# Narrowing float64 weights: the sign bit from GpSimd as a signed zero, and two VectorE steps per tile in place of three

## The chip, the cores and the metric

The kernel runs on one core of one Trainium2 chip. The metric is device time in microseconds (us) of one execution; lower is better. Engines are named as the profile names them: PE is TensorE's matmul and PEld its weight load, DVE is VectorE, ACT is ScalarE, POOL is GpSimd, SP is SyncE, which issues most of the DMAs here.

## The reference

Two attention steps with a small packed set `p` per batch and head (8 batches, 8 heads, 576 rows, 64 columns) are followed by a maxout layer and a softplus layer on all 4608 rows:

```python
p_packed = sm_attn(p, k, v)
out = sm_attn(q, p_packed, p_packed)
...
h = np.maximum(np.maximum(x @ w1, x @ w2), x @ w3)
return (h @ w_out).astype(np.float32)
...
h = x @ w_in
g = np.maximum(h, 0.0) + np.log1p(np.exp(-np.abs(h)))
return (g @ w_out).astype(np.float32)
```

The six weight matrices (`w1`, `w2`, `w3` and `w_out` of the maxout layer, `w_in` and `w_out` of the softplus layer) come in as float64. The kernel has no 64-bit arithmetic, so it reads each number as two 32-bit words and makes a float32 of them itself. That step is called narrowing below, and the change is in it alone.

## The kernel before

A weight tile is 128 partitions by 512 numbers. It lands by DMA in a buffer of pool `stp` (5 buffers) as pairs of words, `raw[:, :, 0]` the low ones and `raw[:, :, 1]` the high ones, so either word alone is read with a step of 8 bytes. ScalarE's `rebase` (L79) reads the high word as a float32 and scales it by 2^-112, which moves the exponent to float32's place and leaves the mantissa three bits too far to the right. VectorE's `narrow` then does three steps: L86 shifts the rebased bits left by three into the high word's place, L89 adds the top three bits of the low word to that, and L97 takes the sign from the rebased value and all other bits from the sum. The buffer is free for the next load after L97.

Fifty-six tiles are narrowed. Eighteen are `w1` to `w3` (the raw tile is named `wraw`, the result stands in `wsb`); tile fw below, such as 32, is block f (0 to 5) of matrix w (0 to 2). Six are `w_out` of the maxout layer (`woraw`, result `wo`), each then split into a high and a low float32r part (`wo_hi` by ACT at L107, `wo_lo` by DVE at L108). These 24 belong to the first 110 us, where a string `order` lists steps by name and gives the order in which they are emitted. The other 32 (`raw`, result `x`) are the softplus layer's weights, narrowed six per batch in the stage that follows (L628 to L632 store and load them) and written back to HBM.

A scheduler places the emitted instructions on each engine's queue, and each queue then runs strictly in its order. The PE work around the change is this. `scores` (L247) makes scores; `attn1_exp` takes their maximum on DVE (L262), scales it (L266, output `ms`) and lets ACT take the exponential (L271). `attn1_transpose` (L286) and `attn1_values` (L306) follow, and DVE divides by the sums (L320, output `pp`); PE transposes `pp` (L231) before it goes on. `packed_weights` (L375, output `ps_w`) multiplies four tiles of `wsb` at a time; group c takes the tiles 4c to 4c+3, counted as 3f+w, so group 2 needs tiles 22, 30, 31 and 32 and group 3 tiles 40, 41, 42 and 50. ACT and DVE split `ps_w` into `pwhi` and `pwlo`. Layer 1 (L396) multiplies with them; its results are evacuated as `m` by ACT (L419) and by DVE (L421, a running maximum), and split into `hhi` and `hlo`. Layer 2 multiplies with `wo_hi` and `wo_lo`. From batch 1 on this repeats about every 59 us; after batch 7, from some 560 us to the end, the softplus layer runs alone.

Of the kernel before, what the change touches and what calls it, by code (L numbers as in the profile page):

```python
# [8 lines left out]
F32 = mybir.dt.float32  # L9
# [3 lines left out]
ALU = mybir.AluOpType  # L13
# [6 lines left out]
def packed_attention_maxout_softplus(  # L20
# [22 lines left out]
    nc = tc.nc  # L43
# [38 lines left out]

    def narrow(raw, x):

        low, high, bits = raw[:, :, 0], raw[:, :, 1], x.bitcast(I32)
        nc.vector.tensor_scalar(  # L86
            out=high, in0=bits, scalar1=3, scalar2=None, op0=ALU.logical_shift_left
        )
        nc.vector.scalar_tensor_tensor(  # L89
            out=high,  # L90
            in0=low,
            scalar=29,
            in1=high,
            op0=ALU.logical_shift_right,
            op1=ALU.bitwise_or,
        )
        nc.vector.scalar_tensor_tensor(  # L97
            out=bits,
            in0=bits,
            scalar=-0x80000000,  # L100
            in1=high,
            op0=ALU.bitwise_and,
            op1=ALU.bitwise_or,
        )

# [359 lines left out]
    def split_wo(f, t):  # L465
        x = mp.tile([P, S], F32, tag="m", name="wo32")
        rebase(t, x[:, :DM])
        narrow(t, x[:, :DM])
        split(x[:, :DM], wo_hi[:, f], wo_lo[:, f])
# [11 lines left out]
    def narrow_w(f, w, t):  # L481
        x = wsb[:, 3 * f + w].rearrange("p c x -> p (c x)")
        rebase(t, x)
        narrow(t, x)
# [137 lines left out]
    def narrow_ahead():  # L622
        if len(in_flight) == AHEAD or not to_narrow and in_flight:
            raw64, dst = in_flight.pop(0)
            x = nwp.tile([P, 512], F32, tag="x32", name="x32")
            rebase(raw64, x)
            narrow(raw64, x)
            nc.sync.dma_start(out=dst, in_=x)  # L628
        if to_narrow:
            src, dst = to_narrow.pop(0)  # L630
            t = stp.tile([P, 512, 2], I32, tag="st", name="raw64")
            nc.sync.dma_start(out=t.rearrange("p n t -> p (n t)"), in_=src)  # L632
            in_flight.append((t, dst))

    for n in range(1, B):
        for slot in range(F1 + KC):
# [21 lines left out]
            if n + 1 == B:  # L658
# [17 lines left out]
                for c, e in [divmod(lot + i, KC) for i in range(2)] if lot is not None else ():  # L676
                    if e == 0:
# [8 lines left out]
                        out=x, in_=wi32[e * P : e * P + P, c * 512 : c * 512 + 512]  # L686
# [177 lines left out]
```

## Time and profile before

| | |
|---|---|
| Time, median of 3 runs | 1338.73 us (1338.31 to 1339.14) |
| The profiled execution, its own time | 1341.63 us |
| Its span, first to last instruction | 1339.8 us |
| PE busy | 1304.5 us, 97% |
| DVE busy | 894.2 us, 67% |
| ACT busy | 617.9 us, 46% |
| POOL busy | 0.7 us, 6 instructions |
| Mean granted clock of PE | 0.993 |

The page sums over the whole span. PE is busy almost throughout, so what counts is where it is not, and which engine's instruction ends each of these gaps; that is read from the waits and from the timeline of the stretch in question. The table by stretches gives for each engine its busy time, the count of instructions in brackets, and the granted clock of PE, 1.00 being the full 2.4 GHz.

### The profile page before, as it was taken

How to read it: one execution, taken by the hardware profiler on the slowest of the kernel's cores; microseconds unless marked ns; L12 is line 12 of the kernel's file. 1: busy time of each engine (PE TensorE's matmuls, PEld its weight loads, DVE VectorE, ACT ScalarE, POOL GpSimd, SP SyncE). 2: the span in 40 equal slices, each digit the busy share in tenths (PEclk: the TensorE clock that was granted, in tenths of full speed). 3: DMA queues.
4: the chain of work that ended last, by engine and by line, in shares of the span. 5: the costliest groups of instructions: out<-in, count | busy, mean ns of one | idle time of the engine just before them, and what ended most of it. 6: DMA issues, size and time to landing. Idle time of an engine off the chain costs nothing.

```text
span 1339.8 us, 21462 instructions
## 1 busy us (share of the span) xinstructions
PE 1304.5 (97%) x8656; PEld 1100.2 (82%) x8656; DVE 894.2 (67%) x1480; ACT 617.9 (46%) x1045; POOL 0.7 (0%) x6
## 2 busy tenths in 40 slices
PE   4889999999999999999999999999999999999998
PEld 3778888898989899788888888888888888888887
DVE  4787778786878746866556566565665665655654
ACT  3544434444443435745445454454444544544443
POOL 0000000000000000000000000000000000000000
PEclk9979999999999999999999999999999999999999
DMA  9873677877577506501102011010020110000101
GB/s 269 214 197 92 170 202 180 208 212 204 178 201 201 134 36 215 159 0 38 26 1 64 0 32 32 0 47 17 4 60 0 32 32 0 24 8 1 32 1 32
DMA packets 61859, 119.17 MB, mean 89 GB/s; under 512 B 11072, under 2 KB 28736, under 8 KB 61760
## 3 DMA queue, kind: packets, MB, share of 16 engines
q1 hardware_dynamic: 55984, 106.66, 29.8%
q10 hardware_dynamic: 5776, 11.14, 2.5%
q8 instruction: 68, 1.11, 0.3%
q14 instruction: 31, 0.25, 0.1%
HBM read 90.51 MB, written 27.26 MB: 88 GB/s over the span
## 4 chain that ended last, share of the span: by engine, by line
PE 89%; DMA 5%; DVE 3%; ACT 1%; issue 1%; SPq 0%; DVEq 0%; ACTq 0%
PE ps L396 55%; PE acc L781 10%; PE acc L780 10%; PE acc L779 10%; PE ps_w L375 2%; DMA wraw<-in_moe_w_dram 1%; DMA wi_x<-wi 1%; PE ps_s L247 1%; PE ps_v L306 1%; PE ps_e L286 1%; DMA x2d<-xs 1%; DMA kraw<-in_k_dram 1%; DMA vt<-in_v_dram 1%; PE ps_k L199 1%; DVE pwlo L108 0%
## 5 line engine op out<-in xcount | busy, mean ns | idle before, releaser
L396 PE MATMUL ps<-x2hi,wilo 128*128 128x512 f32 x576 | 228.0, 396 | 0.0
L396 PE MATMUL ps<-x2lo,wihi 128*128 128x512 f32 x576 | 227.0, 394 | 0.0
L396 PE MATMUL ps<-x2hi,wihi 128*128 128x512 f32 x576 | 226.7, 394 | 0.0
L781 PE MATMUL acc<-w2hi,glo 128*128 128x512 f32 x576 | 226.0, 392 | 0.0
L780 PE MATMUL acc<-w2lo,ghi 128*128 128x512 f32 x576 | 225.7, 392 | 0.0
L779 PE MATMUL acc<-w2hi,ghi 128*128 128x512 f32 x576 | 224.5, 390 | 0.7 <-ACT ghi L107 0.7
L107 ACT ACTIVATE ghi<-t 128x512 fp32r<-128x512 f32 x144 | 91.0, 632 | 289.0 <-DVE t L761 288.6
L754 DVE TENSOR_SCALAR t<-ex 128x512 f32<-128x512 f32 x144 | 61.4, 426 | 161.9 <-ACT ex L751 161.9
L108 DVE TENSOR_TENSOR glo<-t,ghi 128x512 fp32r<-128x512 f32 x144 | 99.7, 692 | 92.6 <-ACT ghi L107 92.5
L396 PE MATMUL ps<-a2hi,pwhi 128*128 128x288 f32 x576 | 129.3, 307 | 2.5 <-ACT a2hi L107 1.3
L779 PEld LDWEIGHTS acc<-w2hi,ghi 128*128 128x128 f32 x576 | 108.2, 188 | 25.8 <-ACT ghi L107 1.2
L396 PEld LDWEIGHTS ps<-x2lo,wihi 128*128 128x128 f32 x576 | 108.1, 188 | 25.8
L396 PEld LDWEIGHTS ps<-x2hi,wilo 128*128 128x128 f32 x576 | 108.3, 188 | 25.2
L750 ACT ACTIVATE ex<-ps 128x512 f32<-128x512 f32 x144 | 86.2, 598 | 92.3 <-PE ps L396 92.2
L780 PEld LDWEIGHTS acc<-w2lo,ghi 128*128 128x128 f32 x576 | 108.1, 188 | 25.0
L396 PEld LDWEIGHTS ps<-x2hi,wihi 128*128 128x128 f32 x576 | 108.1, 188 | 24.5
L781 PEld LDWEIGHTS acc<-w2hi,glo 128*128 128x128 f32 x576 | 108.1, 188 | 23.5 <-DVE glo L108 0.4
L396 PE MATMUL ps<-a2lo,pwhi 128*128 128x288 f32 x576 | 124.3, 298 | 0.7 <-DVE a2lo L108 0.7
L396 PE MATMUL ps<-a2hi,pwlo 128*128 128x288 f32 x576 | 124.2, 297 | 0.0
L757 DVE TENSOR_TENSOR t<-ln,t 128x512 f32<-128x512 f32 x144 | 99.7, 692 | 30.4 <-ACT ln L752 30.4
L396 PEld LDWEIGHTS ps<-a2hi,pwhi 128*128 128x128 f32 x576 | 93.1, 192 | 15.8 <-ACT m L419 5.9
L761 DVE SCALAR_TENSOR_TENSOR t<-ps,t 128x512 f32<-128x512 f32 x144 | 99.5, 691 | 4.7
(90 smaller groups left out, 1847.9 us busy)
## 6 DMA issues: line engine op xcount, KB each, us to landing
qraw<-in_q_dram SPq DMA_DIRECT2D x112, 140.0 KB
kraw<-in_k_dram SPq DMA_DIRECT2D x96, 140.0 KB
wraw<-in_moe_w_dram SPq DMA_DIRECT2D x18, 512.0 KB
x2d<-xs ACTq DMA_DIRECT2D x32, 288.0 KB
x2r<-x2d SPq DMA_DIRECT2D x36, 256.0 KB
out_dram<-o SPq DMA_DIRECT2D x136, 64.0 KB
raw<-in_moe_w_in_dram SPq DMA_DIRECT2D x16, 512.0 KB
raw<-in_moe_w_out_dram SPq DMA_DIRECT2D x16, 512.0 KB
```

What stands on the lines that cost most here:

```text
L107: nc.scalar.activation(out=hi, in_=src, func=AF.Copy)
L108: nc.vector.tensor_tensor(out=lo, in0=src, in1=hi.bitcast(F32), op=ALU.subtract)
L199: nc.tensor.matmul(ps[64 * G : 64 * G + 64, i // hi, c : c + rows], r[:, i, G], ident[:rows, :rows], start=True, stop=True,)
L375: nc.tensor.matmul(ps[cols, G, : units * P].rearrange("p (w x) -> p w x", w=units), ppT[n][rows, cols], wsb[rows, 4 * c : 4 * c + units, g ...
L396: nc.tensor.matmul(o, w, xx, start=first, stop=last)
L750: nc.scalar.activation(out=ex, in_=ps, func=AF.Abs)
L754: nc.vector.tensor_scalar(out=t, in0=ex, scalar1=1.0, scalar2=-1.0, op0=ALU.add, op1=ALU.add)
L757: nc.vector.tensor_tensor(out=t, in0=ln, in1=t, op=ALU.subtract)
L761: nc.vector.scalar_tensor_tensor(out=t, in0=ps, scalar=0.0, in1=t, op0=ALU.max, op1=ALU.add)
L779: nc.tensor.matmul(ps, ghi[:, cols], whi, start=(f == 0), stop=False)
L780: nc.tensor.matmul(ps, ghi[:, cols], wlo, start=False, stop=False)
L781: nc.tensor.matmul(ps, glo[:, cols], whi, start=False, stop=(f == F2 - 1))
```

## The change

Instead of L86, GpSimd multiplies the high word, read as a float32, by 0.0 in place, once `rebase` has read it: what remains is a zero with the number's sign. L89 adds the top three bits of the low word to this and writes the sum to the low word's place. L97 shifts the rebased bits left by three, which drops their sign, and adds the sum. VectorE has two instructions per tile in place of three, GpSimd has one, and L89 waits for GpSimd.

```diff
         low, high, bits = raw[:, :, 0], raw[:, :, 1], x.bitcast(I32)
-        nc.vector.tensor_scalar(
-            out=high, in0=bits, scalar1=3, scalar2=None, op0=ALU.logical_shift_left
-        )
+        zero = high.bitcast(F32)
+        nc.gpsimd.tensor_scalar(out=zero, in0=zero, scalar1=0.0, scalar2=None, op0=ALU.mult)
         nc.vector.scalar_tensor_tensor(
-            out=high,
+            out=low,
             in0=low,
             scalar=29,
             in1=high,
...
             out=bits,
             in0=bits,
-            scalar=-0x80000000,
-            in1=high,
-            op0=ALU.bitwise_and,
+            scalar=3,
+            in1=low,
+            op0=ALU.logical_shift_left,
             op1=ALU.bitwise_or,
```

PE's instructions keep their order. On DVE and ACT the scheduler places the work around the narrowing anew. Three places are shown, each as before and then as changed; names are as in the section on the kernel, with the program's buffer numbers.

DVE, in the first 35 us, where the maxima of batch 1's first scores (`mx`, `ms`) meet the second `wo` tile (`wo_258`). Before:

```order
L262 TENSOR_REDUCE mx<-ps_s 128x1
L86 TENSOR_SCALAR woraw<-wo_258 128x512
L266 TENSOR_SCALAR ms<-mx 128x1
L262 TENSOR_REDUCE mx<-ps_s 128x1
L89 SCALAR_TENSOR_TENSOR woraw<-woraw 128x512
L266 TENSOR_SCALAR ms<-mx 128x1
L315 TENSOR_SCALAR sg<-es 128x1
L97 SCALAR_TENSOR_TENSOR wo_258<-wo_258,woraw 128x512
```

The same stretch of DVE's queue as changed:

```order
L262 TENSOR_REDUCE mx<-ps_s 128x1 x2
L89 SCALAR_TENSOR_TENSOR woraw<-woraw 128x512
L266 TENSOR_SCALAR ms<-mx 128x1 x2
L97 SCALAR_TENSOR_TENSOR wo_258<-wo_258,woraw 128x512
L315 TENSOR_SCALAR sg<-es 128x1
L319 RECIPROCAL rc<-sg 128x1
L108 TENSOR_TENSOR wo_lo<-wo_258,wo_hi 128x512
```

The first `ms`, which stood ahead of this tile's L89, now stands behind it, and `wo_lo` has moved up ahead of the next tile's steps. On ACT, `wo_hi` of this tile has moved ahead of the second exponential.

DVE, around 77 to 84 us, between the two `pwlo` of group 2 and the last tile that group 3 needs (tile 50). Before:

```order
L86 TENSOR_SCALAR wraw<-wsb 128x512
L108 TENSOR_TENSOR pwlo<-ps_w,pwhi 128x512
L89 SCALAR_TENSOR_TENSOR wraw<-wraw 128x512
L421 TENSOR_TENSOR m<-ps_813,m 128x576
L86 TENSOR_SCALAR wraw<-wsb 128x512
L97 SCALAR_TENSOR_TENSOR wsb<-wsb,wraw 128x512
L421 TENSOR_TENSOR m<-ps_828,m 128x576
L89 SCALAR_TENSOR_TENSOR wraw<-wraw 128x512
L86 TENSOR_SCALAR wraw<-wsb 128x512
L97 SCALAR_TENSOR_TENSOR wsb<-wsb,wraw 128x512
```

The same stretch as changed:

```order
L89 SCALAR_TENSOR_TENSOR wraw<-wraw 128x512
L108 TENSOR_TENSOR pwlo<-ps_w,pwhi 128x512
L89 SCALAR_TENSOR_TENSOR wraw<-wraw 128x512
L421 TENSOR_TENSOR m<-ps_813,m 128x576
L97 SCALAR_TENSOR_TENSOR wsb<-wsb,wraw 128x512 x2
L421 TENSOR_TENSOR m<-ps_828,m 128x576
L89 SCALAR_TENSOR_TENSOR wraw<-wraw 128x512
```

The last L97 of the first listing, tile 50's, has moved ahead of the maximum `m<-ps_828`, and its L89 ahead of `m<-ps_813`. Some 8 us ahead of this, tile 31's L89, which stood before the maximum `m<-ps_730`, now stands behind it together with tile 32's.

DVE, around 86 to 89 us, where the results of batch 1's first attention step (`pp`) are made. Before:

```order
L108 TENSOR_TENSOR hlo<-m,hhi 128x576
L108 TENSOR_TENSOR pwlo<-ps_w,pwhi 128x512
L97 SCALAR_TENSOR_TENSOR wsb<-wsb,wraw 128x512
L86 TENSOR_SCALAR woraw<-wo_962 128x512
L108 TENSOR_TENSOR pwlo<-ps_w,pwhi 128x512
L320 TENSOR_SCALAR pp<-ps_v,rc 128x64 x2
```

The same stretch as changed:

```order
L108 TENSOR_TENSOR hlo<-m,hhi 128x576
L108 TENSOR_TENSOR pwlo<-ps_w,pwhi 128x512
L89 SCALAR_TENSOR_TENSOR wraw<-wraw 128x512
L320 TENSOR_SCALAR pp<-ps_v,rc 128x64
L108 TENSOR_TENSOR pwlo<-ps_w,pwhi 128x512
L97 SCALAR_TENSOR_TENSOR wsb<-wsb,wraw 128x512
L320 TENSOR_SCALAR pp<-ps_v,rc 128x64
```

The two `pp` are now apart, with the second `pwlo` and tile 52's L97 between them.

## Rows read from the trace of the kernel before

**Rows 1.** The page: the span, the busy time of each engine, and the granted clock of PE in 40 slices of 33.5 us.

```profile
span 1339.8 us, 21462 instructions
PE 1304.5 (97%) x8656; PEld 1100.2 (82%) x8656; DVE 894.2 (67%) x1480; ACT 617.9 (46%) x1045; POOL 0.7 (0%) x6
PEclk9979999999999999999999999999999999999999
```

**Rows 2.** Busy time by stretches: the stretch, its length, then PE, PEld, DVE, ACT and POOL busy (instructions), the granted clock, the DMA share and GB/s.

```profile
160.00:480.00 320.00, 318.43 (x3279) 287.28 (x3278) 253.57 (x440) 131.71 (x233) 0.00 (x0) 1.00 0.68 183
480.00:560.00 80.00, 79.27 (x556) 71.08 (x555) 50.91 (x81) 45.01 (x80) 0.00 (x0) 1.00 0.45 148
560.00:1340.00 780.00, 775.78 (x3362) 630.85 (x3360) 477.05 (x752) 371.51 (x608) 0.00 (x0) 1.00 0.08 23
```

**Rows 3.** What PE waited for, over the whole span: us in total, times, longest.

```profile
PE ps_w L375 <- DVE wsb L97: 4.9, 2, 2.6
PE ps_t L231 <- DVE pp L320: 2.1, 2, 1.3
PE ps_s L247 <- DVE vT L223: 1.2, 4, 0.3
PE ps L396 <- DVE hlo L108: 0.5, 1, 0.5
```

**Rows 4.** The removed instruction L86 on the 32 late tiles and on the 18 `wsb` tiles, and the step L89, which stays, on the latter: count, shortest, median and longest in ns, and when the first and last started.

```profile
L86 DVE TENSOR_SCALAR raw<-x x32: 374/422/453, 152.3 to 461.8; 128x512 int32<-128x512 int32 x32
L86 DVE TENSOR_SCALAR wraw<-wsb x18: 417/423/430, 13.6 to 84.2; 128x512 int32<-128x512 int32 x18
L89 DVE SCALAR_TENSOR_TENSOR wraw<-wraw x18: 682/693/695, 14.0 to 85.1; 128x512 int32<-128x512 int32 x18
```

**Rows 5.** The timeline of POOL, three of its six instructions: start, us, and what it was.

```profile
0.24 0.10 POOL L842 MEMSET const-float32-0.0<- 128x1 f32 x1 [0.24 <-issue]
...
0.73 0.20 POOL masks.py:197 MEMSET ident<- 128x128 f32 x1 [0.29 <-POOLq L842]
1.01 0.29 POOL masks.py:199 TENSOR_SCALAR_AFFINE_SELECT ident<-ident 128x128 f32<-128x128 f32 x1
```

**Rows 6.** The timeline from 29 to 40 us, all engines: the first place of the change.

```profile
29.57 0.66 ACT L79 ACTIVATE wo<-woraw 128x512 f32<-128x512 f32 x1 [2.38 <-DMA woraw<-in_moe_w_out_dram]
...
30.61 0.15 DVE L266 TENSOR_SCALAR ms<-mx 128x1 f32<-128x1 f32 x1
...
30.87 0.76 ACT L271 ACTIVATE e<-ps_s,ms 128x576 f32<-128x576 f32 x1
31.34 0.68 DVE L89 SCALAR_TENSOR_TENSOR woraw<-woraw 128x512 int32<-128x512 int32 x1
...
35.20 2.79 PE L306 MATMUL ps_v<-vt,e1T 96*32 96x64 f32 x96 [0.26 <-ACT e1T L292]
...
35.75 0.69 ACT L79 ACTIVATE wsb<-wraw 128x512 f32<-128x512 f32 x1
...
38.86 0.28 DVE L320 TENSOR_SCALAR pp<-ps_v,rc 128x64 f32<-128x64 f32 x1
...
39.29 0.45 PE L231 MATMUL ps_t<-ident,pp 128*128 128x128 f32 x1 [1.29 <-DVE pp L320]
```

**Rows 7.** The timelines of DVE, ACT and PE around groups 2 and 3 of the packed weights, in that order.

```profile
69.18 0.76 DVE L421 TENSOR_TENSOR m<-ps,m 128x576 f32<-128x576 f32 x1 [0.71 <-PE ps L396]
...
72.17 0.69 DVE L97 SCALAR_TENSOR_TENSOR wsb<-wsb,wraw 128x512 int32<-128x512 int32 x1
...
79.74 0.76 DVE L421 TENSOR_TENSOR m<-ps,m 128x576 f32<-128x576 f32 x1 [0.67 <-PE ps L396]
80.42 0.42 DVE L86 TENSOR_SCALAR wraw<-wsb 128x512 int32<-128x512 int32 x1
80.75 0.68 DVE L97 SCALAR_TENSOR_TENSOR wsb<-wsb,wraw 128x512 int32<-128x512 int32 x1
81.35 0.75 DVE L421 TENSOR_TENSOR m<-ps,m 128x576 f32<-128x576 f32 x1
...
82.95 0.68 DVE L97 SCALAR_TENSOR_TENSOR wsb<-wsb,wraw 128x512 int32<-128x512 int32 x1
...
77.17 0.58 ACT L107 ACTIVATE pwhi<-ps_w 128x512 fp32r<-128x512 f32 x1
...
78.72 1.22 ACT L79 ACTIVATE wsb<-wraw 128x512 f32<-128x512 f32 x2
...
73.01 1.96 PE L375 MATMUL ps_w<-wsb,ppT 64*32 64x512 f32 x16 [2.34 <-DVE wsb L97]
...
83.78 1.96 PE L375 MATMUL ps_w<-wsb,ppT 64*32 64x512 f32 x16 [2.59 <-DVE wsb L97]
```

**Rows 8.** What followed the second of these waits: the stretch from 83.78 us by busy time and clock (columns as in rows 2), and the timeline of DVE and PE at its end.

```profile
83.78:92.83 9.05, 8.29 (x127) 6.42 (x128) 7.14 (x14) 1.71 (x4) 0.00 (x0) 0.50 1.04 251
...
88.61 0.47 DVE L320 TENSOR_SCALAR pp<-ps_v,rc 128x64 f32<-128x64 f32 x2
...
89.23 0.45 PE L231 MATMUL ps_t<-ident,pp 128*128 128x128 f32 x1 [0.76 <-DVE pp L320]
```

**Rows 9.** The timeline at the last two `wo` tiles, DVE and then PE.

```profile
107.33 0.76 DVE L86 TENSOR_SCALAR woraw<-wo 128x512 int32<-128x512 int32 x2
...
113.61 0.53 PE L396 MATMUL ps<-hlo,wo_hi 128*128 128x288 f32 x2 [0.48 <-DVE hlo L108]
```

## The prediction

> **What bounds the kernel now.** I read the page first. PE is busy 1304.5 of 1339.8 us, so all that any change outside PE can win is the 35.3 us in which it is idle, and what its clock loses: one slice in 40 stands at 0.7 of full speed [rows 1]. Then the table by stretches, to see where the idle time lies. From 160 to 480 us it is 1.6 us, from 480 to 560 us 0.7, from 560 to the end 4.2 [rows 2]; the other 28.8 us lie before 160 us. Of the 56 narrowed tiles 32 belong to the stretch with 1.6 us of idle time, and there DVE itself is busy 253.6 of 320 us, so it has room already. The 24 tiles of the first 110 us are what can matter. Last the waits of PE: two waits for a last narrowing step of `wsb`, 4.9 us together, two for `pp`, 2.1, and one for `hlo`, 0.5 [rows 3]. These 7.5 us are the places where narrowing stands ahead of PE, directly or by filling DVE's queue. I go through them one by one.
>
> **What the parts cost.** Removed: 56 L86 at 0.42 us [rows 4], 23.6 us of DVE's 894. Nearly all of it lies beside other work. The steps that stay keep their shape and their 0.69 us; back to back they start 0.60 us apart (80.75 to 81.35) [rows 7]. Added: 56 GpSimd multiplications of 128x512. No row shows one, so I bound it by the POOL rows there are [rows 5]. A memset takes 0.10 us for one element per partition and 0.20 for 128, which gives 0.10 + 4 x 0.10 = 0.50 us for 512; the affine select, which also reads, takes 0.29 for 128, which gives 0.10 + 4 x 0.19 = 0.86, or 1.16 if nothing of it is fixed. I take 0.86, since it is the one that reads a tile, and keep 0.50 and 1.16. The Trainium skill (GPSIMD Engine Reference, section Performance versus the Vector engine) gives 769 ns for 512 elements of a one-input loop at its best; by that the sum below would be about 0.1 us lower, since only the first place waits for this length alone. So for one tile alone the path from `rebase` to the result becomes longer (0.86 in place of 0.42, and one more hand-over), while DVE's queue becomes shorter. Which of the two counts depends on whether DVE is late or idle when the tile comes.
>
> **First place, 29 to 39 us.** Here DVE's new order costs. The second `wo` tile is rebased at 29.57, so GpSimd would have its sign from 30.3 to about 31.15. Its L89 now stands ahead of both `ms`, so DVE waits for GpSimd, runs L89 from 31.2, and makes the first `ms` at 31.85 in place of 30.61 [rows 6]. The exponential that it releases moves from 30.87 to 31.95. Behind it on ACT stand a rebase, `wo_hi`, the second exponential, another rebase and the two copies of `e1T`, and PE's `ps_v`, which began at 35.20, would begin near 36.15 and end near 38.95. DVE, meanwhile, is less behind: tile 10's rebase comes at about 36.1 (35.75 before), its sign at 37.65, its two steps end at 38.9, and the second `pp` comes at about 39.1 in place of 38.86. PE's transpose would start near 39.5, not 39.29: **+0.2 us**, between -0.2 (a sign step of 0.50) and +1.0 (no slack on ACT). PE passes this on to all that follows.
>
> **Second place, groups 2 and 3.** From the maximum at 69.18 on [rows 7] the new order is: two L89 at 69.85 and 70.45, L97 of tile 31 at 71.05, a maximum at 71.65, L97 of tile 32 at 72.3. Before, that L97 started at 72.17; group 2 gains nothing (+0.15), because tile 31's first step no longer uses the idle time ahead of 69.18. Group 3 gains. Both steps of tile 40, `hlo`, tile 41's steps, the two `pwlo` and tile 42's L89 take DVE to about 78.65; tile 50's rebase now stands ahead of ACT's copy of `m`, right behind the `pwhi` of 77.17 (0.25 us later now, with the DVE work it waits for), so it runs from 78.0 to 78.65 (from 78.72 before), and its sign is there at 79.55. Then L89, the maximum (79.74 before, 80.15 now), and the two L97 at 80.8 and 81.4. The last one before was that of 82.95, because a maximum, another tile's L86 and this tile's own L86 and L89 stood in between. Group 3 would start at 82.25 in place of 83.78. Most of these 1.5 us are lost again 5 us on: PE's `ps_v` ends 1.5 us sooner, but the two `pp` are now apart, with a `pwlo` and an L97 between them, and that `pwlo` needs ACT, which needs the first `pwlo`. I get the second `pp` at 88.25 to 88.55 and PE's transpose at 88.7 in place of 89.23 [rows 8]: **-0.55 us** in all, between +0.5 and -1.5.
>
> **Third place, the last two `wo` tiles.** Two L86, 0.67 us by their starts (107.33 to 108.00), stand in a queue that is full until `hlo`, for which PE waits 0.48 us [rows 9]. The signs can be ready by 107.5, since both tiles are rebased before DVE comes to them. The gain is the whole wait and no more: **-0.5 us**, between 0 and -0.5.
>
> **The 32 tiles after 150 us.** DVE is freed of 13.5 us, which PE's 1.6 us of idle time [rows 2] caps; what it waits for there on DVE is `vT`, 1.2 us [rows 3]. I take -0.3, between 0 and -1.2. Stores of `x` wait longer by the sign step's length, and loads behind them on SP's queue with them, but no wait of PE for a load is among the 1.6 us.
>
> **Sum.** 0.2 - 0.55 - 0.5 - 0.3 = -1.15 us. Against the profiled execution, 1341.6 us (span 1339.8 and 1.8 around it), that is 1340.5; it lies 2.9 us above the median of the runs, so for the median I say 1338.73 - 1.15 = **1337.6 us**. With all the lower ends together it is 1335.3 (-3.4), with all the upper ones 1340.2 (+1.5). About 0.2%, 2.7 us, is what a measurement of this kernel can tell from no change, so the forecast is "same".
>
> **Rival 1, slower: GpSimd's step holds up DVE's.** L89, L97, `hlo` and `wo_lo` each read two tiles from SBUF. If such an instruction and the sign step could not read at once, each step that falls into a full stretch of DVE's queue would hold it for 0.86 us, twice what the removed L86 took. No row can show it: POOL ends at 1.3 us [rows 5], and DVE's first such step (L89, 14.0 us) comes long after [rows 4]. I count the signs that fall into a full queue ahead of a wait of PE: three before 38.86, one before 72.17, four from there to 88.61, two at 107: ten. If half of them meet a two-input step, that is 5 x 0.86 = 4.3 us, 1337.6 + 4.3 = **1341.9 us**; if all ten do, 1346. It decides the sign from a hold of about 0.5 us on five steps on (4 us would be 0.8 each for a measurable loss). The Trainium skill (SBUF — State Buffer, section Who interferes with whom) says just this: a DVE instruction with two SBUF inputs and a GpSimd instruction that reads SBUF exclude each other, and the later one waits for the whole of the other. What speaks against its weight is that many neighbours in these stretches (the maxima, `pwlo`) read one input from PSUM, and that ACT's and PE's waits leave holes. Chance 0.27.
>
> **Rival 2, faster: the clock.** After the 2.59 us wait before group 3 the granted clock stood at 0.50, the 1.2 GHz level, for 9 us [rows 8]; the 9.05 us from 83.78 to 92.83 would take 4.5 at 2.4 GHz. That wait began at 83.78 - 2.59 = 81.19; the forecast shortens it to 82.25 - 81.19 = 1.06 us. If the clock then stays up, 4.5 us more are won: 1337.6 - 4.5 = **1333.1 us**. Against it: group 2's wait of 2.34 us stays, its `ps_w` ran at the same 1.96 us as group 3's [rows 7], and the wait for `pp` behind `ps_v` becomes longer by about as much as the one before group 3 becomes shorter. Chance 0.2.
>
> **Rival 3: the step is far longer than the rows bound.** At 1.5 us or more it would be late at each place and the gains above would go: +1 us, within "same". Chance 0.05, leaving 0.48 for the forecast.
>
> **How the numbers follow.** The forecast's own range is 1335.3 to 1340.2. The range for 8 in 10 reaches to rival 2's time and past rival 1's likely one: 1332.8 to 1343.0. Faster by over 0.2% (below 1336.0): rival 2 and a small part of the forecast's lower end, 0.26. Slower by over 0.2% (above 1341.4): most of rival 1 and its larger counts, 0.25. Within: 0.49.
>
> **What would show it.** A POOL row L88 of 0.5 to 1.2 us, 56 times. PE's wait for `wsb` at L97 at about 3.5 us in place of 4.9, the one before group 3 near 1 us, and the wait for `pp` longer than 2.1. No wait of PE for `hlo` at 113 us. If rival 1 holds, L89, L97 and `hlo` rows of well over 0.7 us stand beside POOL rows, and DVE's busy time does not fall by 23.6 us. If rival 2 holds, the slice of 0.7 in the clock line rises. The forecast is wrong if PE's idle time after 160 us changes by more than 1.6 us, or if a wait of PE for GpSimd appears.

## The result

| | before | changed |
|---|---|---|
| median of the runs (lowest to highest) | 1338.93 us (1338.31 to 1339.88, 4 runs) | 1356.78 us (1355.14 to 1357.52, 4 runs) |
| profiled execution, its span | 1341.63, 1339.8 us | 1356.51, 1354.7 us |
| DVE busy | 894.2 us | 883.6 us |
| POOL busy | 0.7 us | 92.3 us |

The ratio is 1.013, 95% interval 1.0117 to 1.0142: 17.9 us slower. The forecast was 1337.6 us, "same", in a range of 1332.8 to 1343.0; it is wrong in size and direction.

The page of the changed kernel, to be read beside [rows 1]:

```profile
span 1354.7 us, 21630 instructions
PE 1302.7 (96%) x8656; PEld 1098.9 (81%) x8656; DVE 883.6 (65%) x1424; ACT 616.1 (45%) x1045; POOL 92.3 (7%) x62
PEclk7779999999999999999999999999999999999999
```

PE does as much work as before, in a longer span, so it waits more. DVE gave back 10.6 us and not the 23.6 us of 56 L86 [rows 4]. Part of that difference is in the counting: steps back to back start before the one ahead has ended [rows 7], and in two kernels below that also lack L86 and have no reads on GpSimd (e1, e8) DVE's busy time falls by 18.3 us. The instructions themselves, from the views of the lines L88, L89 and L97: count, shortest, median and longest in ns, first and last start:

```profile
L88 POOL TENSOR_SCALAR raw<-raw x32: 1539/1568/2110, 158.4 to 477.2; 128x512 f32<-128x512 f32 x32
L88 POOL TENSOR_SCALAR wraw<-wraw x18: 1532/1568/2097, 13.3 to 89.7; 128x512 f32<-128x512 f32 x18
L89 DVE SCALAR_TENSOR_TENSOR raw<-raw x32: 649/692/1139, 160.0 to 478.8; 128x512 int32<-128x512 int32 x32
L89 DVE SCALAR_TENSOR_TENSOR wraw<-wraw x18: 677/694/1129, 14.8 to 92.0; 128x512 int32<-128x512 int32 x18
L97 DVE SCALAR_TENSOR_TENSOR wsb<-wsb,wraw x18: 674/692/1130, 16.1 to 93.4; 128x512 int32<-128x512 int32 x18
```

GpSimd's step takes 1.57 us, 1.8 times what the forecast took and above its upper bound of 1.16. The medians of DVE's steps are as before, but the longest here are 1.13 to 1.14 us; the longest L89 of `wsb` was 0.695 [rows 4]. What PE waited for, and what DVE waited for on POOL (us in total, times, longest), to be read beside [rows 3]:

```profile
PE ps L396 <- DVE m L421: 8.4, 6, 1.7
PE ps_t L231 <- DVE pp L320: 6.8, 2, 4.2
PE ps_e L286 <- ACT e L271: 6.0, 2, 5.8
PE ps_w L375 <- DVE wsb L97: 5.7, 2, 4.3
...
PE ps L396 <- DVE hlo L108: 1.1, 1, 1.1
...
DVE raw L89 <- POOL raw L88: 24.8, 17, 2.3
DVE wraw L89 <- POOL wraw L88: 24.3, 12, 14.8
```

The first line is new: a maximum `m` after 160 us, for which PE had no wait from 160 to 480 us before. The `pp` wait has gone from 2.1 to 6.8, the `wsb` wait from 4.9 to 5.7, the `hlo` wait from 0.5 to 1.1. None names POOL, since PE never waits for POOL itself; but DVE waits for it 29 times on the tiles of these two kinds.

Where the time is lost shows in a landmark that returns in each batch, a stretch of 156 matmuls without a wait. From the chain of work that ended last (start, us, what), first before, then changed:

```profile
168.63 20.98 PE ps L396 x156
227.83 20.98 PE ps L396 x156
...
465.36 20.97 PE ps L396 x156
```

```profile
175.68 21.05 PE ps L396 x156
236.81 21.06 PE ps L396 x156
...
480.97 21.06 PE ps L396 x156
```

In these two traces 7.05 us are lost ahead of the first landmark. After it the five steps to the sixth take 305.29 us in place of 296.73, 8.56 more, 1.7 for each batch. So there are two losses, of early tiles and of late ones, about as large as each other. The first figure is rough: in the traces of six kernels with the early tiles narrowed as before (before itself and, below, e2, e7, e9, e10 and e12) the first landmark stands anywhere from 163.80 to 168.63. The distance from landmark to landmark has no such spread: 59.2 to 59.4 us in before, e10 and e12.

The early loss begins in the first place. DVE, POOL and PE there, and behind them PE at the second place (its waits before groups 2 and 3 and for `pp`) and at the third, from the timeline (start, us, what, and in brackets the idle time ahead of it and what ended it):

```profile
32.05 0.20 DVE L266 TENSOR_SCALAR ms<-mx 128x1 f32<-128x1 f32 x2
...
37.52 1.11 DVE L89 SCALAR_TENSOR_TENSOR wraw<-wraw 128x512 int32<-128x512 int32 x1 [0.42 <-POOL wraw L88]
...
39.34 1.12 DVE L89 SCALAR_TENSOR_TENSOR wraw<-wraw 128x512 int32<-128x512 int32 x1
40.57 0.69 DVE L97 SCALAR_TENSOR_TENSOR wsb<-wsb,wraw 128x512 int32<-128x512 int32 x1
41.18 0.47 DVE L320 TENSOR_SCALAR pp<-ps_v,rc 128x64 f32<-128x64 f32 x2
...
35.55 5.28 POOL L88 TENSOR_SCALAR wraw<-wraw 128x512 f32<-128x512 f32 x3 [0.23 <-ACT wsb L79]
...
41.80 0.45 PE L231 MATMUL ps_t<-ident,pp 128*128 128x128 f32 x1 [2.66 <-DVE pp L320]
...
77.39 1.96 PE L375 MATMUL ps_w<-wsb,ppT 64*32 64x512 f32 x16 [4.30 <-DVE wsb L97]
...
87.70 1.09 PE L375 MATMUL ps_w<-wsb,ppT 64*32 64x512 f32 x16 [1.44 <-DVE wsb L97]
...
94.42 0.45 PE L231 MATMUL ps_t<-ident,pp 128*128 128x128 f32 x1 [4.15 <-DVE pp L320]
...
119.62 0.53 PE L396 MATMUL ps<-hlo,wo_hi 128*128 128x288 f32 x2 [1.08 <-DVE hlo L108]
```

The first `ms` comes at 32.05, close to the 31.85 of the forecast. Then three signs in a row keep POOL from 35.55 to 40.83, each L89 can start only behind its sign, and both `pp` stand behind the second of these tiles in DVE's queue: 41.18, and PE starts at 41.80 in place of 39.29 [rows 6]. In the second place PE's transpose starts at 94.42 in place of 89.23 [rows 8]; at the third PE goes on at 119.62 in place of 113.61 [rows 9].

The late loss, shown in the batch around 295 us, from the timelines of ACT, POOL, DVE and PE:

```profile
292.90 1.22 ACT L79 ACTIVATE x<-raw 128x512 f32<-128x512 f32 x2
...
293.70 3.09 POOL L88 TENSOR_SCALAR raw<-raw 128x512 f32<-128x512 f32 x2 [5.54 <-ACT x L79]
...
295.31 1.13 DVE L89 SCALAR_TENSOR_TENSOR raw<-raw 128x512 int32<-128x512 int32 x1 [1.54 <-POOL raw L88]
296.53 0.69 DVE L97 SCALAR_TENSOR_TENSOR x<-x,raw 128x512 int32<-128x512 int32 x1
297.14 0.75 DVE L421 TENSOR_TENSOR m<-ps,m 128x576 f32<-128x576 f32 x1
...
297.95 0.53 PE L396 MATMUL ps<-hhi,wo_hi 128*128 128x288 f32 x2 [1.67 <-DVE m L421]
```

The rebase comes just ahead of the sign, DVE stands at L89 for 1.54 us with nothing else to do, and the maximum, which needs no sign, stands behind it in the queue. PE waits 1.67 us for that maximum. The L89 itself, beside the second sign, takes 1.13 us in place of 0.69, so up to 0.44 of the 1.67 us can come from there.

### The profile page after: what moved, and what is told of

The parts are those of the page before. It is cut to its first block, busy times and chain, and to the rows that moved or that the text cites. A ratio compares the mean times of both kernels' runs of the same rounds, so it can differ in the third digit from the quotient of the medians.

```text
span 1354.7 us, 21630 instructions
## 1 busy us (share of the span) xinstructions
PE 1302.7 (96%) x8656; PEld 1098.9 (81%) x8656; DVE 883.6 (65%) x1424; ACT 616.1 (45%) x1045; POOL 92.3 (7%) x62
## 4 chain that ended last, share of the span: by engine, by line
PE 83%; DVE 3%; DMA 2%; issue 2%; POOL 1%; ACT 1%; SPq 1%; POOLq 0%; DVEq 0%; ACTq 0%
PE ps L396 52%; PE acc L781 10%; PE acc L780 10%; PE acc L779 10%; DMA kraw<-in_k_dram 1%; PE ps_w L375 1%; POOL raw L88 1%; DVE m L421 1%; DMA raw<-in_moe_w_in_dram 1%; PE ps_e L286 1%; PE ps_s L247 0%; DVE raw L89 0%; DVE pwlo L108 0%; ACT x L79 0%; DMA wraw<-in_moe_w_dram 0%
```

## The experiments

**How long GpSimd's step takes by itself.** Before's kernel, with GpSimd operations of several sizes on an unused part of `wsb` in the first 12 us; b is 128x1024, a its numbers in pairs.

```
+        nc.gpsimd.memset(b, 0.0)
+        nc.gpsimd.memset(a[:, :, 1], 0.0)
+        for t in (a[:, :, 1], a[:, :256, 1], b[:, :512], b):
+            nc.gpsimd.tensor_scalar(out=t, in0=t, scalar1=0.0, scalar2=None, op0=ALU.mult)
+        nc.gpsimd.tensor_copy(b[:, :512], b[:, 512:])
```

> The kernel before, with eight GpSimd instructions of other forms on an unused tile in its first 12 us, where VectorE is idle, so nothing is in their way: memsets of 1024 packed and of 512 spaced numbers, the multiplication by 0.0 on 512 spaced, 256 spaced, 512 packed and 1024 packed numbers, and a copy of 512. Theory W: the multiplication on 512 spaced numbers takes about 1.55 us alone, as in the changed kernel, so its length is its own and not a wait for VectorE; rival C: alone it takes under 1.1 us. If the time goes by numbers, 256 takes about half and 1024 twice as long; if the spacing costs, 512 packed numbers are much cheaper.

The groups of POOL in that run, by shape (busy us, mean ns):

```profile
L112 POOL TENSOR_SCALAR wsb<-wsb 128x512 f32<-128x512 f32 x2 | 3.0, 1512 | 0.2
L112 POOL TENSOR_SCALAR wsb<-wsb 128x1024 f32<-128x1024 f32 x1 | 2.8, 2769 | 0.1
...
L112 POOL TENSOR_SCALAR wsb<-wsb 128x256 f32<-128x256 f32 x1 | 0.9, 876 | 0.1
L113 POOL COPY wsb<-wsb 128x512 f32<-128x512 f32 x1 | 0.6, 611 | 0.1
L110 POOL MEMSET wsb<- 128x512 f32 x1 | 0.5, 549 | 0.0
```

The multiplication's length is its own: DVE has no instruction in this stretch. The first group holds one of spaced and one of dense numbers; the timeline has them at 1.54 and 1.49 us, so spacing costs next to nothing. From 256 to 512 spaced numbers it grows by 0.66 us, from 512 to 1024 dense ones by 1.28, so about 2.5 ns for each number and 0.2 us fixed. A copy of 512, which also reads, takes 0.61, a memset 0.55. So the bounds of the forecast fit a memset and a copy, and not this instruction. The Trainium skill (GPSIMD Engine Reference, section Performance versus the Vector engine) gives 769 ns for 512 elements of a tight loop without branches, its best case; the 1512 ns here are twice that.

**The same queues with a short step.** The sign step is replaced, first by a memset of the high word, then by a copy of it onto itself; the order of DVE's queue stays that of the changed kernel.

```
-        nc.gpsimd.tensor_scalar(out=zero, in0=zero, scalar1=0.0, scalar2=None, op0=ALU.mult)
+        nc.gpsimd.memset(zero, 0.0)             # e1_memset
+        nc.gpsimd.tensor_copy(zero, zero)       # e5_copy
```

> The changed kernel with every queue in the same order, but GpSimd's step is a memset of the high word in place of the multiplication, so all weights lose their sign (this part of the computation is left out). A memset writes and does not read; by the rows of before I estimate 0.50 us for it in place of the 1.57 us that the multiplication took. Theory W (VectorE's queue waits for the 1.57 us step): 1337 to 1341 us, VectorE's wait for GpSimd at L89 well under half of the 50 us of the changed kernel. Rival F (the two-step form and the new order of the queues cost the 18 us): 1354 to 1358 us. Rival C (VectorE and GpSimd hinder each other's reads) gives the same fall as W here and is told apart by other runs.

> The changed kernel with every queue in the same order, GpSimd's step being a copy of the high words onto themselves, so the words keep exponent and mantissa and the weights come out wrong (the sign step is left out). A copy of 512 numbers took 0.61 us, a memset 0.55 us: almost the same length, but the copy reads. Theory W (the length of the step, waited for in VectorE's queue, is what costs): 1336 to 1339 us, as with the memset. Rival C (VectorE and GpSimd hinder each other's reads): 1342 us or more, and L89 to L97 longer than 0.70 us in the mean.

With the memset (0.566 us by the median) the run takes 1336.36 us, ratio 0.9979 (0.9966 to 0.9992); with the copy (0.656) 1340.52, ratio 1.0015 (1.0005 to 1.0026). In both the distance from landmark to landmark is 59.4 us, as before. The copy's run is near the forecast's places: PE's transpose at 38.91 and 88.41, where it said 39.5 (at earliest 39.1) and 88.7. The memset's run is 0.6 us below the range of theory W and inside the forecast's own range of 1335.3 to 1340.2. The copy's misses the latter by 0.3, and lies between theory W and rival C; by its ratio it is 2.0 us slower than before, where the forecast had 1.15 faster. So the step of 1.57 us, by its length and by whatever its reads add, made up nearly all of the 17.9 us. One sign of theory W did not come: with the memset DVE's waits for POOL are 28.7 us, not well under half of the 49.1 shown above; 14.1 of these are one wait.

Between memset and copy lie 4.2 us and only 0.09 us of length, and their intervals do not overlap. DVE is busy 875.9 and 882.1 us, the longest L89 or L97 takes 0.72 and 1.18 us, and the copy's longest L88 is 1.64 us. The Trainium skill (SBUF — State Buffer, section Who interferes with whom) has a VectorE instruction with two inputs from SBUF collide with a GpSimd instruction that reads SBUF and not with one that only writes it; these lengths agree. Whether such collisions make the 4.2 us is not shown. The first landmark (165.11 and 167.90) is 2.8 us apart, inside the spread of the six kernels above, and the granted clock differs too, 1.00 and 0.85 from 92 to 100 us. After that landmark the distances do not differ, 59.4 us for both, though the copy lengthens L89 and L97 there as well (to 1.12 and 1.16 us).

A kernel with the signs' reads beside the old three steps, and no wait for them (e6), gave no result.

**The two halves apart.** Early tiles or late ones keep the three VectorE steps (`narrow3` is the function of before).

```
-        narrow(t, x[:, :DM])
-        narrow(t, x)
+        narrow3(t, x[:, :DM])       # e2_late_only: both early calls
+        narrow3(t, x)
...
-            narrow(raw64, x)
+            narrow3(raw64, x)       # e3_early_only: the late call alone
```

> Only the 32 late tiles are narrowed the new way; the 24 tiles of the first 110 us keep the three VectorE steps. In the trace of the changed kernel PE is 6.0 us late at 113.6 us of before, and 14.9 us late at the end, so 8.9 us arise behind the first 24 tiles. Theory W: each batch from 1 to 6 loses 1.5 to 1.9 us where two late tiles follow each other and a maximum (L421) stands behind the waiting L89; 1338.9 + 9 = 1348 us (1346 to 1351). If the late tiles only pass on a delay of the first ones: 1339 us.

> Only the 24 tiles of the first 110 us are narrowed the new way, the 32 late ones the old way. Theory W: 1338.9 + 6 to 9 = 1345 to 1348 us, with the waits of PE for pp and for the second exponential as in the changed kernel. The two halves of the change should add up to about 18 us with the run before this.

Late only: 1346.71 us, ratio 1.0058 (1.0037 to 1.008). Early only: 1348.17, ratio 1.0071 (1.0052 to 1.0089). Worked out on 1338.9 us that is +7.8 and +9.5, together 17.3 of the 17.9, so within their intervals the halves add up. Late only has PE wait for `m` 8.0 us in 5 times, which is the whole of its loss, and 61.1 us from landmark to landmark; early only has 59.4, with the first landmark at 177.54. In that run the clock granted from 20 to 42 us is 0.98, and 0.50 in the changed kernel's profile; PE's transpose at the first place comes late at either level (42.48 and 41.80), so the lower digits at the start of the clock line are not its cause.

**The form without GpSimd.** The same arithmetic, the multiplication on VectorE.

```
-        nc.gpsimd.tensor_scalar(out=zero, in0=zero, scalar1=0.0, scalar2=None, op0=ALU.mult)
+        nc.vector.tensor_scalar(out=zero, in0=zero, scalar1=0.0, scalar2=None, op0=ALU.mult)
```

> The changed kernel's arithmetic (high word made a signed zero, then two steps), but with the multiplication on VectorE, so three VectorE steps and nothing on GpSimd. If GpSimd's step is the cause (its length, its reads or the wait for it), the time is that of before: 1336 to 1341 us, with a DVE row L88 of about 0.4 us 56 times. If the new form or the order of the rebase, which this step no longer reads, were the cause, it would stay above 1345.

1339.49 us, ratio 1.001 (1.000 to 1.0021), L88 on DVE 0.42 us. The new form costs at most 2.8 us, and by the median 1.3; what costs is this multiplication on GpSimd. With the multiplication on ScalarE instead (a copy scaled by 0.0; the zero then comes out without its sign, so this kernel leaves the signs out):

> The two VectorE steps of the change, with the signed zero made by ScalarE (a scaled copy by 0.0, about 0.67 us as the rebase) right after the rebase, and none on GpSimd. Theory W, by the same sum as for a short GpSimd step: 1336 to 1339 us, since ScalarE is busy under half of the first 160 us. Against it: 56 x 0.67 = 37 us more on ScalarE's queue, where pwhi and hhi stand behind; if these become late, 1341 us or more.

1337.97 us, ratio 0.999 (0.9981 to 0.9999). Taking L86 off DVE (875.9 us busy in place of 894.2) for 56 more instructions of ACT is again "same".

**The late loss: wait or collision?** Five kernels with the early tiles as before. In the first, the rebase and the sign are written one slot of the loop ahead of the two VectorE steps.

```
+        if signed:
+            raw64, x, dst = signed.pop(0)
+            finish(raw64, x)
+            nc.sync.dma_start(out=dst, in_=x)
...
             rebase(raw64, x)
-            narrow(raw64, x)
-            nc.sync.dma_start(out=dst, in_=x)
+            sign(raw64)
+            signed.append((raw64, x, dst))
```

> The 32 late tiles narrowed the new way, the 24 first the old way (as in the run that took 1346.7), but each late tile's rebase and sign step are issued one slot (about 10 us) ahead of its two VectorE steps. The step keeps its 1.57 us and its reads. Theory W: VectorE no longer waits for GpSimd at L89, the 8 us of PE's waits for a maximum (L421) go, and the time is 1337 to 1340 us. Rival C: the collisions stay, 1344 us or more.

1350.48 us, ratio 1.0087 (1.0071 to 1.0104): no better than e2. But its trace shows that the edit did not do what it was meant to: DVE still waits 24.2 us for POOL, in 17 times, since the scheduler put rebase, sign and L89 (here L95) together again. So the next kernel also queues the two steps behind the second maximum of their slot (`m_last`), and a control does the same with the old three steps.

```
+            with tc.issue_after(m_last[0]):
+                finish(raw64, x)            # e9; e10: narrow(raw64, x) of before
```

> The 24 early tiles as before (three VectorE steps); the 32 late tiles with the sign from GpSimd, but rebased and signed one slot of the loop before the two VectorE steps, and these two queued behind the second maximum of that later slot, so that pp and the maxima no longer stand behind an L89 that waits. Theory A (VectorE's queue: what costs in the late tiles is that maxima and pp wait behind a waiting L89): PE's wait for DVE m falls from 8.0 us in 5 times to under 3, the time from layer work to layer work returns from 61.2 to 59.4 to 59.8 us, and the run takes 1337 to 1341 us (ratio 0.998 to 1.002). Theory B (collisions of the two engines in SBUF cost it): the same reads take place, the time from batch to batch stays near 61 and the run takes 1344 to 1348 us. Theory C (length of the path of a tile to its store): later still, over 1348.

> A control for e9: the kernel before with its three VectorE steps for the late tiles put at the same place (rebased a slot ahead, the steps behind the second maximum), with nothing on GpSimd. Under every theory about GpSimd it takes the time of before, 1336 to 1341 us; if it is faster by over 3 us, a gain of e9 would be one of the place and not of the wait that went.

The control takes 1338.98, ratio 1.0004 (0.9993 to 1.0015): the place costs nothing. e9 takes 1349.21, ratio 1.0077 (1.0065 to 1.0089), just above theory B's range and in theory C's. But the waits tell more than the time:

```profile
PE ps_w L404 <- DVE m L450: 8.2, 5, 1.9
...
DVE raw L95 <- POOL raw L91: 13.2, 10, 1.5
```

DVE's waits for POOL fell from 23.4 us (17 times, e2) to 13.2 (10 times), and PE lost as much as ever. The waits that went were free; those that stayed are two in each batch, shown here in the timeline of DVE, with PE's wait behind the second:

```profile
277.94 0.69 DVE L95 SCALAR_TENSOR_TENSOR raw<-raw 128x512 int32<-128x512 int32 x1 [1.15 <-POOL raw L91]
278.72 0.69 DVE L103 SCALAR_TENSOR_TENSOR x<-x,raw 128x512 int32<-128x512 int32 x1
279.33 0.47 DVE L349 TENSOR_SCALAR pp<-ps_v,rc 128x64 f32<-128x64 f32 x2
279.72 1.61 DVE L450 TENSOR_TENSOR m<-ps,m 128x576 f32<-128x576 f32 x2
...
284.38 1.13 DVE L95 SCALAR_TENSOR_TENSOR raw<-raw 128x512 int32<-128x512 int32 x1 [1.54 <-POOL raw L91]
285.60 0.69 DVE L103 SCALAR_TENSOR_TENSOR x<-x,raw 128x512 int32<-128x512 int32 x1
286.21 0.75 DVE L450 TENSOR_TENSOR m<-ps,m 128x576 f32<-128x576 f32 x1
...
287.02 1.09 PE L404 MATMUL ps_w<-wsb,ppT 64*32 64x512 f32 x16 [1.86 <-DVE m L450]
```

At both a rebase on ACT comes just ahead of the sign of the same tile; `pp` and two maxima stand behind the first waiting L95, and the maximum for which PE waits behind the second. The last two kernels take these two waits away and put them back: two slots of distance and four buffers for `x32`, then two slots with the three buffers of before.

```
-        if signed:
+        while len(signed) == 2 or signed and not in_flight and not to_narrow:
...
-    nwp = a_ctx.enter_context(tc.tile_pool(name="nwp", bufs=3))
+    nwp = a_ctx.enter_context(tc.tile_pool(name="nwp", bufs=4))     # e12 alone
```

> As e9, but the two VectorE steps come two slots of the loop behind the rebase and the sign, and x32 has four buffers in place of three, so that the rebase does not wait for a store. In the two places of each batch where PE still waited in e9 (an L95 ahead of pp and two maxima, an L95 ahead of a maximum), VectorE's queue now has the maxima first, or a tile whose sign was made long before. The same 32 signs read SBUF on GpSimd. Theory A (only those two waits of a batch, with maxima behind them in VectorE's queue, cost time): PE's wait for DVE m falls from 8.2 us to under 1.5, from layer work to layer work 59.4 to 59.7 us, and the run takes 1337.5 to 1341.5 us (ratio 0.999 to 1.002). Theory B (the collisions of two engines in SBUF cost it): 1345 to 1350 us as in e2 and e9.

> As e12, but with three buffers for x32 again. A rebase then has to wait until the store three tiles back is done, and in the two places of each batch ScalarE rebases the same tile whose L95 stands next in VectorE's queue, ahead of pp and the maxima. Theory A: the two waits of each batch are back, PE's wait for DVE m near 8 us, 61 us from layer work to layer work, 1345 to 1350 us. If instead it was only the two slots of distance that helped in e12, 1337 to 1341 us.

With four buffers 1338.67 us, ratio 0.9995 (0.9985 to 1.0004); with three 1349.76, ratio 1.0087 (1.0053 to 1.0122), and there PE waits for `m` 8.1 us in 5 times. In e12, what PE waited for from 160 to 480 us, all of it:

```profile
PE ps_s L276 <- DVE vT L252: 1.2, 4, 0.3
PE ps L425 <- DVE pwlo L137: 0.2, 1, 0.2
```

Its chain of work, two landmarks 59.37 us apart:

```profile
224.84 20.98 PE ps L425 x156
284.21 20.98 PE ps L425 x156
```

And the views of its lines of the sign step (L91) and of the two VectorE steps (L95, L103):

```profile
L91 POOL TENSOR_SCALAR raw<-raw x32: 1541/1582/1982, 149.3 to 459.6; 128x512 f32<-128x512 f32 x32
...
L95 DVE SCALAR_TENSOR_TENSOR raw<-raw x32: 648/683/698, 164.4 to 461.7; 128x512 int32<-128x512 int32 x32
...
L103 DVE SCALAR_TENSOR_TENSOR x<-x,raw x32: 648/693/1151, 165.1 to 462.9; 128x512 int32<-128x512 int32 x32
```

32 signs of 1.58 us, and PE waits only 1.4 us in 320. The late loss is gone although the signs and their collisions are still there: by the timelines five steps of late tiles take 1.1 us or more in e12 (L103), as in e2 (L89), e9 and e13 (L95). So what cost was a maximum behind a step that waits for its sign, not the step or its reads by themselves; with a longer path from a tile to its store than e9's, e12 speaks against theory C too. How much the lengthened step adds where the queue waits, no run separates.

## Why the prediction was wrong, step by step

- **What bounds the kernel**: right. PE sets the time, DVE's freed time is worth next to nothing, and with a step that is short and reads nothing on GpSimd (e1, e8) taking L86 away gave 1 to 3 us.
- **The step that failed first: the price of the multiplication.** 0.86 us was taken, 0.50 to 1.16 as bounds, from memsets and an affine select of at most 128 numbers. It is 1.57. A row for another operation on another size did not bound this one, and "below 1.16" was treated as near certain.
- **The step that made it costly: Rival 3.** It was there, with its condition of 1.5 us, a chance of 0.05 and a price of +1 us, "the gains above would go". The whole change cost 17.9 us. That sentence counted the gains that vanish, and left out the work that stands behind a waiting L89 in DVE's queue: both `pp`, and the maxima.
- **First place**: the start was met (`ms` at 32.05 for 31.85), but by luck: the `wo` tile was rebased at 28.14 in place of 29.57, its sign was done at 30.56, and L89 stood behind two maxima (`mx`) and did not wait for GpSimd. The forecast then gave the second `pp` at 39.1 and had tile 10's sign done by 37.65; this sign was the second of three in a row and done at 39.0, and with the lengthened L89 behind it both `pp` came from 41.18 on. +0.2 became +2.5 us. With the copy's 0.656 us the transpose came at 38.91, so -0.4.
- **Second place**: -0.55 in all was forecast; PE's transpose of `pp` came 5.2 us late, 2.5 of them from the first place, so 2.7 were lost here. The wait before group 2 rose from 2.34 to 4.30 us; the one before group 3 fell to 1.44, where 1.06 was forecast; the one for `pp` rose to 4.15. With the copy the transpose is 0.8 early (88.41 against 89.23).
- **Third place**: the wait for `hlo` was to vanish; it is 1.1 us, and PE goes on 6.0 us later than before. Of these only 0.8 (6.0 less 5.2) were lost there.
- **The 32 late tiles**: -0.3 was forecast, between 0 and -1.2, with DVE's room as the reason. The room is an average. The same view shows DVE busy 253.6 of 320 us [rows 2], and does not show that once in each batch a maximum for which PE then waits stands behind a tile's steps. Loss: 7.8 us alone (e2). PE's idle time from 160 to 480 us went from 1.6 to 9.4 us, which is the change after 160 us that the prediction had named as a sign of being wrong.
- **Rival 1 (the shared reads)**: one sign came, DVE steps of 1.1 us beside POOL rows; such a step was held 0.44 us, not the whole step of 0.86 that was counted. The other sign, that DVE's busy time does not fall by 23.6 us, did not tell: it falls by 18.3 with no reads on GpSimd (e1, e8), so only 7.7 of the missing 13.0 us can be from collisions. As a cause of the 17.9 us it holds for a part at most: in the late tiles the collisions by themselves cost nothing (e12). How the 9.5 us of the early tiles divide between the step's length and the reads stays open: no run had a long step without reads in the same queue order, and the memset and the copy do not settle it.
- **Rival 2 (the clock)**: only its first half came. After the shorter wait `ps_w` of group 3 ran in 1.09 us in place of 1.96; but the wait for `pp` behind it grew, as the prediction had held against this rival, and from 92 to 100 us the granted clock was 0.57 (0.90 before). The line of the granted clock fell, from 9979 to 7779 in its first four slices, and e3 has the early loss with 9889.

## What to carry to other kernels

An instruction moved to another engine can be paid for twice: by its own length there, and by everything that stands in the queue of the engine that now waits for it. So before a step is moved to an engine with room, read which instructions stand right behind its consumer in that queue, and whether PE or a transfer waits for one of these; e12 shows that distance between the step and its consumer, with the buffers that this needs, takes the whole loss of the late tiles away, and gains nothing over the kernel before. And the price of an operation is measured for that operation and size, or its bound is left wide.

## What was not expected of the hardware

- GpSimd's multiplication by a constant took about 2.5 ns for each number of a partition, 1.5 us for 512; a copy and a memset of 512 numbers took 0.61 and 0.55 us in all (e4).
- In the changed kernel's timeline, a VectorE instruction with two inputs from SBUF that began 0.06 to 0.1 us after such a step took 1.10 to 1.14 us in place of 0.69 (once 1.24), about 0.44 more; where it began with POOL's step or up to 0.4 us ahead of it, POOL's step took 1.75 to 2.11 us in place of 1.57. The Trainium skill (SBUF — State Buffer, section Who interferes with whom) calls this an exclusive lock of the shared ports and says, of VectorE's 2-port modes, that whoever issues first has them for the whole instruction and the other is fully blocked. The trace does not agree for these two-input steps: the L89 of 295.31 began beside the second of the signs that run to 296.79, and had ended, at 296.44, before it (a profile's times on POOL are rough).
- ScalarE's scaled copy with a scale of 0.0 gave a zero without the sign of its input (e8; inferred: its output is off by the same relative error, 20636.17, as with the memset's plain zeros in e1), where GpSimd's and VectorE's multiplication keep it.
